# Batch 1's a*b as Strassen's block products in a fused attention and expert kernel

## The chip, the cores and the metric
The kernel runs on one core of one Trainium2 chip. The metric is the device time of one execution in microseconds. PE is TensorE, ACT ScalarE, DVE VectorE, POOL GpSimd; SP issues the DMAs.

## What is computed
The reference in short (B, H, S, D = 2, 8, 576, 64; all float32):

```
attention: local = softmax(causal(q k^T / 8)) v
           mem = (phi(q) M_prev) / (phi(q) z_prev + 1e-6),  phi(x) = max(x, 0) + min(exp(x), 1)
           x = sigmoid(beta) mem + (1 - sigmoid(beta)) local      -> 1152 x 512
first part: a = x w1;  b = x w2;  h = (a * b) w3;  x' = h w_out    (weights arrive as float64)
experts:    out = sum over e of p[:, e] * (relu(x' w1[e]) w2[e]),  4 experts, F = 1024
```

## The kernel before
Products of float32 precision are made from two fp32r numbers, a high and a low half, in three passes (PASSES: high by low, low by high, high by high). "Splitting" a tile is a cast on ACT (or POOL) and a subtraction on DVE (`lo_dve`) or POOL (`lo_pool`).

Attention runs over 8 pairs of heads, p = 0 to 7; pairs 0 to 3 are batch 0. Its steps have short names: e, f (phi), s (scores), m (row peak on DVE), x (exp on ACT), t, c (transposes on PE, copies on ACT), v (product with v), j (scaling), n, g (the memory product and its scaling), ja (the sum of both, on POOL), z, zh, zl (the transposed x, high and low half). Pairs 0 to PLAIN - 1 have their scores from plain float32 q and k; for the others q and k are split first (hq, hk on ACT, lq, lk on POOL).

Beside it the weights are converted: o units are w_out, w units the product W = w3 w_out (so h w_out is hT by W), b units the tiles of w1 and w2. Each unit has ACT operations (oa, wa, ba), joins on DVE (od, wd, bd) and splits (oh and ol; wp; bp). b<u>_<a> is batch 0's a or b for weight tile u and half a of the 576 tokens: 12 matmuls of 288 columns. bc keeps a in SBUF; rm, rh, rl multiply and split the result into hT. k and kc are batch 0's c = hT by W and its copy to x2, in two PSUM banks M0 and M1 (one for each half). As a tile of w1 or w2 is joined for batch 0 it is stored to DRAM (wf), and read again for batch 1.

The string FIRST lists these steps in an order written out by hand. Inside `tc.manual_schedule(engines=...)` the named engines execute their instructions in the program's order; what is issued outside, or on an engine not named, a planner puts between by its own costs. In FIRST, SP is not named: loads of the ring of staging buffers are issued by `ahead()` at the joins, the loads of q, k and v (loadq, loadk, head) at their steps.

Then batch 1's a*b (`BUnits`, lines 493 to 582): 16 weight tiles, each loaded from wf, split by ACT and DVE, and used in 2 x 12 matmuls of 288 columns; `times`, `h_hi`, `h_lo` make hT. In between `early` splits two of the experts' operand blocks and prepares the first expert weight set. Batch 1's c (`c1`, line 839) is issued outside the order, so the planner places it.

The expert stage (lines 919 to 962) already works by Strassen's scheme in its Winograd form: for a pair of weight tiles seven block products P1 to P7 of 6 matmuls (two k blocks, three passes), summed in the PSUM banks Z, Q and R. `prep_1` (line 744) makes the weight operands of a set from a raw tile r: hi0 to hi3 are casts on ACT, lo0 to lo3 subtractions on POOL, s31 and s24 two sums or differences each on POOL. hi0 and lo0 split A11 and A12; s31 makes S3 and S1; s24 makes S2 and S4 and overwrites the raw A11 and A12, after lo0.

Of the kernel before, what the change touches and what calls it, by code (L numbers as in the profile page):

```python
# [19 lines left out]
e0 f0 s00 s01 m00 m01 s02 x00 s03 loadq2 loadk2 m02 x01 m03 wa0 t00 t02 c00 wd0 x02 s10 wp0 c02 x03 e1 t04 m10 oa0 t01  # L20
f1 c04 s11 x10 od0 t05 s12 c01 c05 m11 t03 e2 t06 oa1 m12 v00 c03 od1 s13 loadq3 loadk3 c06 x11 v01 m13 x12 v02 head4
head5 x13 t10 oa2 j0 t11 s20 c10 od2 c11 s21 hq3 t14 m20 hk3 lq3 t12 c14 m21 c12 n0 x20 lk3 loadk5 t13 g0 v10 c13 x21
f2 v11 oh0 ja0 e3 t15 oh2 t16 s22 c15 ol0 c16 oh1 t20 m22 wa1 v12 head6 head7 t22 ol1 x22 s23 loadq4 loadk4 j1 w0_0
c20 m23 c22 t21 n1 wd1 x23 t24 c21 z0 g1 oa3 wp1 t23 w0_1 c24 c23 s30 f3 loadq5 zh0 t25 zl0 ja1 t26 e4 m30 c25 v20 c26
od3 x30 v21 ol2 wa2 s31 v22 head8 head9 m31 oh3 w0_2 j2 x31 s32 wd2 t30 z1 c30 m32 t32 wa3 ol3 zh1 n2 wd3 x32 w0_3
w1_0 c32 zl1 wp2 wa4 t34 g2 s33 c34 t33 m33 y0 ja2 n3 c33 t31 x33 w1_1 wd4 hq4 t35 c31 z2 hk4 g3 lq4 c35 t36 w1_2 zh2
w1_3 f4 loadq6 c36 wa5 v30 zl2 wp3 y1 v31 e5 wd5 v32 head10 head11 w2_0 j3 lk4 loadk6 wa6 w2_1 w2_2 f5 w2_3 w3_0 wd6
y2 w3_1 e6 w3_2 wp4 w3_3 s40 y3 ja3 oa4 w4_0 m40 w4_1 od4 x40 z3 w4_2 wp5 zh3 w4_3 oh4 zl3 s41 y4 s42 m41 wp6 wa7 w5_0
m42 x41 w5_1 w5_2 wd7 x42 w5_3 w6_0 ol4 ba0 wp7 w6_1 y5 w6_2 w6_3 bd0 w7_0 y6 w7_1 oa5 bp0 w7_2 w7_3 s43 y7 od5 b0_0
hq5 hk5 m43 lq5 loadq7 oh5 b0_1 ba1 ol5 x43 lk5 loadk7 t40 t41 bc00 n4 c40 bd1 c41 t44 bc01 t42 c44 g4 bp1 s50 oa6 t43  # L30
m50 v40 c42 c43 od6 x50 b1_0 f6 oh6 b1_1 ba2 ol6 rm00 e7 bd2 t46 t45 rh00 v41 c45 rl00 ba3 rm01 bp2 s51 rh01 m51 c46
v42 head12 head13 rl01 x51 b2_0 bd3 j4 ba4 bp3 b2_1 bc20 s52 bd4 bc21 b3_0 m52 ja4 ba5 b3_1 rm10 x52 bp4 rh10 s53 rm11
rl10 rh11 b4_0 bd5 hk6 hq6 rl11 b4_1 oa7 m53 bp5 x53 t50 bc40 t51 od7 bc41 b5_0 c50 c51 lq6 oh7 b5_1 ba6 rm20 ol7 rh20
bd6 t52 t54 c52 n5 c54 rl20 ba7 rm21 bp6 t53 g5 v50 rh21 c53 t55 rl21 bd7 b6_0 c55 f7 t56 wa8 v51 bp7 c56 bc60 b6_1
# [21 lines left out]
def kernel(  # L56
# [228 lines left out]

    def stage_b(p):
# [27 lines left out]
        def pv(x):  # L314
            def f():
                if x == 0:
                    st["a"] = slots("a")
# [8 lines left out]
            return f
# [733 lines left out]
```

## Time and profile before

| | us |
|---|---|
| median of 3 runs (696.35 to 697.58) | 697.29 |
| profiled execution | 696.56 |
| its span, first to last instruction | 694.4 |
| PE busy | 678.9 |
| DVE, ACT, POOL busy | 415.2, 371.1, 358.7 |

Attention and batch 0's a*b end near 212 us, batch 0's c is 212 to 237, batch 1's a*b 237 to 301 with most of batch 1's c between, and the experts fill the rest. PE's busy time counts matmuls that overlap in the pipeline, so a busy PE can still run at less than its rate; for a rate, starts are to be compared.

### The profile page before, as it was taken

What the parts mean: (1) busy time and instruction counts of PE and PEld (TensorE: products, weight loads), DVE (VectorE), ACT (ScalarE), POOL (GpSimd) and SP (SyncE); (2) the same over time, 40 slices, a digit from 0 to 9 for tenths busy, and PEclk for the clock granted to TensorE, in tenths of its full rate; (3) what the DMA queues carried; (4) which work ended last, traced back from release to release, by engine and by line L of the source; (5) the groups of instructions that cost most, each with busy time, mean ns of one, the idle gap of its engine ahead of it and who ended that gap; (6) DMA issues with size and microseconds to landing.
All of it is one profiled execution on the core that took longest, in us unless ns stands there. A gap on an engine that the chain in (4) does not pass through costs nothing.

```text
span 694.4 us, 12951 instructions
## 1 busy us (share of the span) xinstructions
PE 678.9 (98%) x4999; PEld 610.7 (88%) x4999; DVE 415.2 (60%) x784; ACT 371.1 (53%) x787; POOL 358.7 (52%) x352
## 2 busy tenths in 40 slices
PE   7899999999999999999999999999999999999997
PEld 4678798977999999999898999998999899999896
DVE  6689788898761044456766573455563465634563
ACT  7788686676732134445454544445544445444551
POOL 2225546565450000515767776568765768666660
PEclk9999999999999999999999999999999999999999
DMA  9743256533540013122131322131313122312501
GB/s 302 254 146 102 67 198 195 172 122 123 194 140 31 1 61 122 35 88 93 35 117 61 122 94 89 61 122 62 122 61 121 61 94 90 123 60 85 173 31 60
DMA packets 43404, 74.53 MB, mean 107 GB/s; under 512 B 14416, under 2 KB 14416, under 8 KB 43344
## 3 DMA queue, kind: packets, MB, share of 16 engines
q1 hardware_dynamic: 43344, 73.72, 32.3%
q8 instruction: 39, 0.64, 0.4%
q14 instruction: 21, 0.17, 0.1%
HBM read 67.15 MB, written 6.55 MB: 106 GB/s over the span
## 4 chain that ended last, share of the span: by engine, by line
PE 87%; DMA 4%; DVE 3%; ACT 2%; issue 1%; POOL 1%; SPq 0%; ACTq 0%; POOLq 0%; DVEq 0%
PE o L885 27%; PE Z L932 14%; PE ab L532 13%; PE c L625 7%; PE Q L932 7%; PE wacc L463 6%; PE R L932 3%; PE a L322 2%; PE pt L300 2%; DMA qd<-in_q_cols_dram 2%; PE sc L250 1%; DMA wr<-in_moe_w_tiles_dram 1%; PE b L355 1%; DVE P L266 1%; PE a L332 1%
## 5 line engine op out<-in xcount | busy, mean ns | idle before, releaser
L102 POOL TENSOR_TENSOR w<-r,w 128x512 fp32r<-128x512 f32 x96 | 131.4, 1369 | 186.6 <-ACT w L760 172.8
L885 PE MATMUL o<-w,he 128*128 128x512 f32 x864 | 223.1, 391 | 0.0
L885 PEld LDWEIGHTS o<-w,he 128*128 128x128 f32 x864 | 153.5, 188 | 23.4
L532 PE MATMUL ab<-xT,ws 128*128 128x288 f32 x768 | 107.6, 297 | 1.2 <-POOL ws L102 1.2
L870 ACT ACTIVATE he<-t 128x320 fp32r<-128x320 f32 (+1 forms) x96 | 42.7, 445 | 121.9 <-DVE t L961 74.2
L532 PEld LDWEIGHTS ab<-xT,ws 128*128 128x128 f32 x768 | 103.0, 188 | 2.9 <-POOL ws L102 1.6
L871 DVE SCALAR_TENSOR_TENSOR he<-t,he 128x320 fp32r<-128x320 f32 (+1 forms) x96 | 58.7, 611 | 49.1 <-ACT he L870 49.1
L105 DVE TENSOR_TENSOR w<-r,w 128x512 fp32r<-128x512 f32 x64 | 66.0, 1032 | 0.0
L954 DVE TENSOR_TENSOR t<-u,Q 128x320 f32<-128x320 f32 (+1 forms) x32 | 14.5, 454 | 81.4 <-ACT u L952 81.2
L760 ACT CAST w<-r 128x512 fp32r<-128x512 f32 x96 | 58.9, 614 | 0.0
L625 PE MATMUL c<-hT,W 128*128 128x288 f32 (+2 forms) x384 | 52.9, 295 | 0.0
L625 PEld LDWEIGHTS c<-hT,W 128*128 128x128 f32 x384 | 51.6, 189 | 0.0
L932 PE MATMUL Z<-X0T,w 128*128 128x320 f32 x288 | 50.3, 310 | 0.3 <-ACT s L942 0.3
L932 PEld LDWEIGHTS Z<-X0T,w 128*128 128x128 f32 x288 | 46.0, 188 | 4.2 <-ACT s L942 0.7
L463 PE MATMUL wacc<-wo,w3s 128*128 128x512 f32 x192 | 49.0, 402 | 0.0
L932 PEld LDWEIGHTS Z<-X1T,w 128*128 128x128 f32 x288 | 40.8, 188 | 3.9
L463 PEld LDWEIGHTS wacc<-wo,w3s 128*128 128x128 f32 x192 | 34.7, 188 | 8.2 <-issue 0.6
L932 PE MATMUL Z<-X1T,w 128*128 128x256 f32 x288 | 41.9, 281 | 0.0
L266 DVE CUSTOM_DVE_ANT_0 P<-sc,mask 128x128 f32<-128x128 f32 (+4 forms) x72 | 33.7, 515 | 10.2 <-PE sc L250 9.6
L790 ACT CAST w<-r 128x512 fp32r<-128x512 f32 x64 | 39.5, 618 | 0.0
L271 ACT ACTIVATE P<-P,mn 128x128 f32<-128x128 f32 (+4 forms) x72 | 37.3, 580 | 2.1 <-DVE mn L266 2.0
L99 POOL TENSOR_SCALAR w3s<-tf_l 128x512 fp32r<-128x512 f32 x16 | 11.8, 741 | 51.3 <-DVE tf_l L135 32.4
(136 smaller groups left out, 1157.8 us busy)
## 6 DMA issues: line engine op xcount, KB each, us to landing
r<-in_moe_w_tiles_dram SPq DMA_DIRECT2D x64, 256.0 KB, 3.7
r<-in_moe_w_dram SPq DMA_DIRECT2D x64, 256.0 KB, 2.9
w3r<-in_moe_w_tiles_dram SPq DMA_DIRECT2D x16, 512.0 KB, 3.7
wr<-in_moe_w_tiles_dram SPq DMA_DIRECT2D x16, 512.0 KB, 3.6
wor<-in_moe_w_out_dram SPq DMA_DIRECT2D x8, 512.0 KB, 5.0
wf<-tf SPq DMA_DIRECT2D x16, 256.0 KB, 2.2
wr<-wf SPq DMA_DIRECT2D x16, 256.0 KB, 2.8
qd<-in_q_cols_dram SPq DMA_DIRECT2D x8, 352.0 KB, 3.7
```

The costliest lines, as they stand in the source:

```text
L102: nc.gpsimd.tensor_sub(dst, src, r32(hi))
L105: nc.vector.tensor_sub(dst, src, r32(hi))
L266: nc.vector.tensor_tensor_reduce(out=Pt[i, x], in0=src, in1=mask[:, 0:S] if i == NB else mask[:, S + P - w : S + P], scale=ISCALE, scalar= ...
L463: nc.tensor.matmul(wacc[u], lhsT=w3s[u][:, a, c, :], rhs=wo[4 * g + c][:, bb, :], start=(c == 0 and x == 0), stop=(c == 3 and x == 2),)
L532: nc.tensor.matmul(ps[:, 0:HS], lhsT=self.ws[u][:, wi, kk, :], rhs=xT[b, kk][:, xi, a * HS : (a + 1) * HS], start=(n == 0), stop=(n == 3 * ...
L625: nc.tensor.matmul(st["ps"], lhsT=Wt[kk][:, wi, d * P : (d + 1) * P], rhs=hT[kk][:, xi, t0 : t0 + tw], start=(kk == 0 and x == 0), stop=(k ...
L760: return lambda: nc.scalar.copy(st["w"][i][:, 0], src(i))
L790: return lambda: nc.scalar.copy(w2s[s][x][:, 0], st["r"][:, x])
L870: nc.scalar.activation(h[:, 0], src, AF.Relu)
L871: nc.vector.scalar_tensor_tensor(out=h[:, 1], in0=src, scalar=0.0, in1=r32(h[:, 0]), op0=ALU.max, op1=ALU.subtract)
L885: nc.tensor.matmul(o_ps[i], lhsT=h_of[s][x][:, a, i * P : (i + 1) * P], rhs=w2s[s][x][:, b, :], start=first, stop=last,)
L932: nc.tensor.matmul(ps, lhsT=w1s[s][a][:, wi, kk, :], rhs=X[c, b][:, xi, kk, :], start=first and kk == 0 and x == 0, stop=(kk == 1 and x == ...
```

## The change
- FIRST is written anew, with SP's instructions in it: tokens with @ are loads (@q, @k, @V for two heads, @o, @w, @b, @mz, @bt), bs the stores to wf. SP is now one of the named engines. `gates` is a step of its own, after @bt.
- PLAIN is 4.
- The slots of a pair's nine output blocks are reordered, so that `mem` makes four products of 130 columns over 128 rows and two of 65, and the gates' tiles are smaller.
- For batch 1 `fin_hi` writes x in float32 (two tiles xf), and there is no low half.
- What stands behind the last step of FIRST that is not k (`cut_at`) is issued in a second block together with `work`: `x_b1` makes the seven token operands (B11, B21, B22, T1 to T4) of batch 1's x, and `prep_b1(0..2)` three weight sets. Two entries of `work` follow each k step.
- In that block follow, for m = 0 to 7, the seven products of pair m of weight tiles (w1's tile m is the upper block row, w2's the lower one, the two halves of 576 tokens are the block columns, so the four sums are a and b of either half), with prep_b1(m + 2) for m = 1 to 5 between them. Z and Q of even m are in M0 and M1 with R in o0; those of odd m are in o1, o2, o3.
- The raw tiles of wf have two buffers (the tags of the later blocks X0B22 and X1B22); the sets have three (the experts' v tags, and the tags of T1 to T4 of either part), so these blocks of the experts are allocated after a*b.

```diff
+@q0 @k0 @k1 @q1 e0 @V0 f0 s00 s01 @w0 m00 e1 m01 s02 x00 @o0 f1 s03 @V1 x01 m02 wa0 t00 @k2 t02 m03 @q2 s10 x02 wd0
+@w1 s11 c00 wp0 c02 t01 m10 @o1 x03 t04 c01 s12 @o2 c04 m11 x10 t03 m12 v00 @mz c03 x11 t05 @bt v01 c05 x12 t06 t10
+s13 c06 c10 e2 v02 m13 @q3 oa0 t14 gates j0 @k3 t13 c14 n0 @V2 x13 od0 t11 s20 g0 c11 @o3 wa1 t12 m20 v10 ja0 c12 c13
+x20 t16 v11 f2 oh0 wd1 t15 e3 s21 c15 ol0 @w2 c16 oa1 v12 m21 wp1 w0_0 j1 @V3 x21 s22 od1 s23 m22 t20 oa2 @w3 t22 m23
...
-PLAIN = 3
+PLAIN = 4
...
+    def slot(i, x):
+
+        return i // 2, (i % 2) * 2 + x
...
-                    nc.tensor.matmul(
-                        m[x][:, i], lhsT=phi_t[p][o, i * P : (i + 1) * P], rhs=mz[o, p, x], start=True, stop=True
-                    )
-            for x, o in enumerate(halves):
+                g, s = slot(i, 0)
                 nc.tensor.matmul(
-                    m[0][o, NB], lhsT=phi_t[p][o, NB * P : S], rhs=mz[o, p, x], start=True, stop=True
+                    m[g][:, s : s + 2], lhsT=phi_t[p][:, i * P : (i + 1) * P], rhs=mz[:, p], start=True, stop=True
+                )
+            for x in range(2):
+                nc.tensor.matmul(
+                    m[0][x * SB : (x + 1) * SB, NB], lhsT=phi_t[p][:, NB * P : S], rhs=mz[:, p, x], start=True, stop=True
                 )
 
         def mem_out():
@@ -372,23 +381,26 @@
             nc.gpsimd.tensor_add(st["q"], st["q"], st["m"])
 
...
-            nc.scalar.copy(xT[b, h // 2][:, 0, :], st["x"])
+            nc.scalar.copy(xf[h // 4][:, h // 2 % 2, :] if b else xT[b, h // 2][:, 0, :], st["x"])
 
         def fin_lo():
-            lo_dve(xT[b, h // 2][:, 1, :], st["x"], xT[b, h // 2][:, 0, :])
+            if b == 0:
+                lo_dve(xT[b, h // 2][:, 1, :], st["x"], xT[b, h // 2][:, 0, :])
 
...
+            self.raw[u] = self.flt[u] = from64_join(*self.raw[u])
+
+        def store(self, u):
             wf[u] = wd.tile([P, KD, P], F32, tag=f"f{u}", name=f"wf{u}")
-            nc.sync.dma_start(out=wf[u], in_=f)
-            ahead()
+            nc.sync.dma_start(out=wf[u], in_=self.flt.pop(u))
...
+    for c, n in (("o", KF), ("w", NU), ("b", NU)):
+        parts.update({f"@{c}{u}": lambda c=c, u=u: loads[c](u) for u in range(n)})
+    parts["@bt"] = lambda: nc.sync.dma_start(out=bt, in_=beta)
+    parts["@mz"] = lambda: nc.sync.dma_start(out=mz, in_=m_z)
...
+    cut_at = max(i for i, f in enumerate(FIRST) if f[0] != "k") + 1
+    with tc.manual_schedule(engines=ENGINES | {ET.SP}):
+        for f in FIRST[:cut_at]:
             parts[f]()
...
+    BX = {}
+    b1_raw, b1_set = {}, {}
+
+    def load_b1(m):
+        if m < KF:
+            b1_raw[m] = r = px.tile([P, 2, KD, P], F32, tag=f"X{m % 2}B22", name=f"wr1_{m}")
+            for x in range(2):
+                nc.sync.dma_start(out=r[:, x], in_=wf[2 * m + x])
+
+    def b1_tiles(m):
+        if m % 3 == 0:
+            return [px.tile([P, 2, n, P], F32R, tag=f"v{i}", name=f"b1w{i}_{m}") for i, n in enumerate(SIZES)]
+        c = m % 3 - 1
+        return [px.tile([P, 2, n, P], F32R, tag=f"X{c}{BL[2 + i]}", name=f"b1w{i}_{m}") for i, n in enumerate(SIZES)]
+
+    def prep_b1(m):
+
+        p = prep_1(m, b1_raw, b1_set, b1_tiles, "tb")
+        sub, add = nc.vector.tensor_sub, nc.vector.tensor_add
+        return [
+            lambda: (p["begin"](), p["hi0"]()), p["s31"], p["lo0"], p["hi2"], p["s24"], p["lo2"], p["hi3"], p["lo3"],
+            p["hi1"], lambda: (p["lo1"](), load_b1(m + 2)),
+        ]
+
+    def x_b1():
+
+        x0, x1 = xf
+        t = pf.tile([P, 2, HS], F32, tag="asb", name="xt", bufs=1)
+        lft, rgt = slice(0, HS), slice(HS, S)
+        b11, b12, b21, b22 = x0[:, :, lft], x0[:, :, rgt], x1[:, :, lft], x1[:, :, rgt]
+        where = {
+            "B11": (main, "g6"), "T1": (main, "g7"), "B21": (main, "g2"), "B22": (main, "g3"), "T2": (px, "X0B11"),
+            "T3": (px, "X0B21"), "T4": (main, "g4"),
+        }
+
+        def hi(n, src):
+            def f():
+                pool, tag = where[n]
+                BX[n] = pool.tile([P, 2, 2, HS], F32R, tag=tag, name=f"BX{n}")
+                nc.scalar.copy(BX[n][:, 0], src)
+            return f
+
+        def lo(n, src):
+            return lambda: lo_dve(BX[n][:, 1], src, BX[n][:, 0])
+
+        sub = nc.vector.tensor_sub
+        return [
+            hi("B11", b11), lambda: sub(t, b12, b11), lo("B11", b11), hi("T1", t), lambda: sub(b12, b22, b12), lo("T1", t),
+            hi("B21", b21), hi("B22", b22), lambda: sub(t, b22, t), lo("B21", b21), hi("T2", t), lo("B22", b22),
+            hi("T3", b12), lo("T2", t), lambda: sub(b21, b21, t), lo("T3", b12), hi("T4", b21), lo("T4", b21),
+        ]
+
+    st_m = {}
+
+    def b1_prods(m):
+
+        st_m[m] = st = {}
+        banks = ((psM, "M0"), (psM, "M1"), (ps3, "o0")) if m % 2 == 0 else ((ps3, "o1"), (ps3, "o2"), (ps3, "o3"))
+
+        def new(i):
+            pool, tag = banks[i]
+            return pool.tile([P, 512], F32, tag=tag, name=f"{'ZQR'[i]}b{m}", bufs=1)[:, 0:HS]
+
+        def prod(d, a, b, first):
+            def f():
+                if first:
+                    st[d] = new("ZQR".index(d))
+                for kk in range(2):
+                    for x, (wi, xi) in enumerate(PASSES):
+                        nc.tensor.matmul(
+                            st[d], lhsT=b1_set[m][a][:, wi, kk, :], rhs=BX[b][:, xi, kk, :],
+                            start=first and kk == 0 and x == 0, stop=(kk == 1 and x == 2), skip_group_check=True,
+                        )
+            return f
+
+        def keep(i):
+            def f():
+                if i == 0:
+                    st["u"] = pf.tile([P, 3, HS], F32, tag="ws", name=f"u{m}")
+                nc.scalar.copy(st["u"][:, i], st["Z"])
+            return f
+
+        def add(i, k, d):
+            def f():
+                if i == 0:
+                    st["t"] = pf.tile([P, 3, HS], F32, tag="raw", name=f"t{m}")
+                nc.vector.tensor_add(st["t"][:, i], st["u"][:, k], st[d])
+            return f
+
+        def fin_h(a):
+            def f():
+                t = st["t"]
+                nc.vector.tensor_mul(t[:, a], t[:, a], st["Z"] if a == 0 else t[:, 2])
+                if a:
+                    hT[m] = po.tile([P, 2, S], F32R, tag=f"o{m}", name=f"hT1_{m}")
+                    both = t[:, 0:2].rearrange("p a s -> p (a s)")
+                    nc.scalar.copy(hT[m][:, 0, :], both)
+                    lo_dve(hT[m][:, 1, :], both, hT[m][:, 0, :])
+            return f
+
+        return {
+            "P1": [prod("Z", "A11", "B11", True), keep(0)], "P2": [prod("R", "A12", "B21", True), add(0, 0, "R")],
+            "P6": [prod("Z", "S2", "T2", False), keep(1)], "P5": [prod("Q", "S1", "T1", True)],
+            "P7": [prod("Z", "S3", "T3", False), keep(2), add(2, 2, "Q")], "P4": [prod("Z", "A22", "T4", False), fin_h(0)],
+            "P3": [prod("Q", "S4", "B22", False), add(1, 1, "Q"), fin_h(1)],
+        }
+
+    tail = FIRST[cut_at:]
+    work = x_b1()
+    for m in range(3):
+        work += prep_b1(m)
     with tc.manual_schedule(engines=ENGINES | {ET.SP}):
-        for u in range(NU):
-            pre, m0, m1, post = b1.unit(u)
-            pre()
-            if u == 6:
+        load_b1(0), load_b1(1)
+        per = -(-len(work) // max(1, sum(f[1] != "c" for f in tail)))
+        for f in tail:
+            parts[f]()
+            if f[1] != "c":
+                for g in work[:per]:
+                    g()
+                work = work[per:]
+        for g in work:
+            g()
+        hT.clear()
+        early = [f for k, n in enumerate(("B11", "B21")) for f in split_x(n, 1, block(0, k, 1))]
+        p0 = prep_1(0)
+        early += [
+            lambda: (p0["begin"](), p0["hi0"]()), *(p0[n] for n in ("lo0", "s31", "hi2", "hi3", "s24", "lo2", "hi1", "lo3", "lo1")),
+        ]
+        order = [b1_prods(m) for m in range(KF)]
+        for n in ("P1", "P5", "P2"):
+            for f in order[0][n]:
+                f()
+        for m in range(KF):
+            todo = prep_b1(m + 2) if m and m + 2 < KF else []
+            if m == 4:
                 load_1(0), load_1(1)
-            m0()
-            if u >= 3 and early:
-                early.pop(0)()
-            m1()
-            post()
-            if u >= 8 and early:
-                early.pop(0)()
+            nxt = order[m + 1] if m + 1 < KF else {}
+            seq = [order[m].get("P6"), *([order[m]["P5"]] if m else []), order[m]["P7"], nxt.get("P1"), order[m]["P4"], nxt.get("P2"), order[m]["P3"]]
+            for fs in seq:
+                for f in fs or []:
+                    f()
+                for f in todo[:2]:
+                    f()
+                todo = todo[2:]
+                if early and (m == KF - 1 or m == KF - 2 and len(early) > 10):
+                    early.pop(0)()
+        x_tiles(0, BL[:2])
+        for k, n in enumerate(("B11", "B21")):
+            early += split_x(n, 0, block(0, k, 0))
...
```

## Rows read from the trace of the kernel before
**Rows 1.** Busy time by stage: stretch, length, busy of each engine (instructions), clock, DMA.
```profile
0.00:60.00 60.00, 50.09 (x589) 37.78 (x589) 45.69 (x133) 47.97 (x95) 14.43 (x25) 1.00 0.69 226
60.00:150.00 90.00, 88.85 (x848) 76.65 (x847) 75.29 (x160) 66.43 (x129) 52.81 (x45) 1.00 0.44 142
150.00:211.90 61.90, 61.62 (x594) 54.35 (x593) 46.71 (x94) 36.09 (x71) 29.77 (x28) 1.00 0.41 139
211.90:237.33 25.43, 25.43 (x194) 25.43 (x194) 1.52 (x3) 3.75 (x9) 0.00 (x0) 1.00 0.06 21
...
340.00:694.00 354.00, 350.56 (x2057) 316.13 (x2055) 192.21 (x309) 169.72 (x382) 232.70 (x229) 1.00 0.27 89
```

**Rows 2.** PE in order of time around batch 1's a*b: start, duration (us).
```profile
246.71 1.92 PE L625 MATMUL c<-hT,W 128*128 128x320 f32 x12
248.46 6.53 PE L532 MATMUL ab<-xT,ws 128*128 128x288 f32 x48
254.83 1.92 PE L625 MATMUL c<-hT,W 128*128 128x320 f32 x12
```

**Rows 3.** Waits of PE in the first 60 us: total, times, longest.
```profile
PE a L322 <- ACT pT L304: 2.0, 1, 2.0
...
PE b L355 <- DVE mn L266: 1.3, 2, 1.0
...
PE sc L250 <- DMA kd<-in_k_cols_dram: 1.0, 1, 1.0
...
PE sc L250 <- DVE mn L266: 0.8, 1, 0.8
```

**Rows 4.** ACT in order of time, 20 to 23 us.
```profile
20.84 0.68 ACT L213 ACTIVATE ex<-qd 128x576 f32<-128x576 f32 x1 [3.16 <-DMA qd<-in_q_cols_dram]
...
22.52 0.72 ACT L304 COPY pT<-pt 128x512 f32<-128x512 f32 x2
```

**Rows 5.** Groups of PE: scores with three passes (ks), plain (kd), memory product (mz).
```profile
L250 PE MATMUL sc<-ks,qs 64*128 64x128 f32 (+3 forms) x120 | 13.1, 342 | 0.0
L355 PE MATMUL b<-mz,phi 64*128 64x65 f32 x128 | 8.9, 278 | 1.3 <-DVE mn L266 1.3
L250 PE MATMUL sc<-kd,qd 64*128 64x128 f32 (+3 forms) x48 | 8.5, 465 | 1.8 <-DMA kd<-in_k_cols_dram 1.0 <-DVE mn L266 0.8
```

**Rows 6.** POOL in order of time, one set of the experts' weights.
```profile
279.83 1.89 POOL L767 TENSOR_TENSOR t<-r 128x256 f32<-128x256 f32 x2
281.68 1.43 POOL L768 TENSOR_TENSOR r<-r 128x256 f32<-128x256 f32 x2
283.07 0.73 POOL L772 TENSOR_TENSOR r<-r 128x256 f32<-128x256 f32 x1
283.88 0.86 POOL L773 TENSOR_TENSOR r<-r 128x256 f32<-128x256 f32 x1
284.70 1.29 POOL L102 TENSOR_TENSOR w<-r,w 128x512 fp32r<-128x512 f32 x1
286.15 0.75 POOL L102 TENSOR_TENSOR w<-t,w 128x256 fp32r<-128x256 f32 x1 [0.16 <-ACT w L760]
```

**Rows 7.** ACT in order of time in batch 1's a*b.
```profile
242.62 0.43 ACT L551 CAST hT<-asb 128x288 fp32r<-128x288 f32 x1 [1.15 <-DVE asb L546]
...
246.90 0.40 ACT L542 COPY asb<-ab 128x288 f32<-128x288 f32 x1 [1.20 <-PE ab L532]
247.20 0.62 ACT L523 CAST ws<-wr 128x512 fp32r<-128x512 f32 x1
```

**Rows 8.** DVE in order of time, 206 to 286 us.
```profile
206.07 0.76 DVE L105 TENSOR_TENSOR xT<-x,xT 128x576 fp32r<-128x576 f32 x1 [1.04 <-ACT xT L388]
...
242.12 0.46 DVE L546 TENSOR_TENSOR asb<-ab,asb 128x288 f32<-128x288 f32 x1
...
283.68 0.46 DVE L105 TENSOR_TENSOR hT<-asb,hT 128x288 fp32r<-128x288 f32 x1 [0.50 <-ACT hT L551]
...
285.28 1.03 DVE L105 TENSOR_TENSOR hT<-asb,hT 128x288 fp32r<-128x288 f32 x1 [0.50 <-ACT hT L551]
```

More of the change, by code (lines that the diff above doesn't have):

```diff
@@ L19 @@
 FIRST = """
[L20 to L34, printed above, removed]
@@ L646 @@
         define(p)
-        parts.update({f"load{nm}{p}": lambda nm=nm, p=p: load(nm, p) for nm in "qk"})
-        parts.update({f"head{n}": lambda n=n: load_head(n) for n in (2 * p, 2 * p + 1)})
+        parts.update({f"@{nm}{p}": lambda nm=nm, p=p: load(nm, p) for nm in "qk"})
+        parts[f"@V{p}"] = lambda p=p: (load_head(2 * p), load_head(2 * p + 1))
     for c in range(KF):
@@ L668 @@
             parts[f"kc{d}{a}"] = fs[4]
-    with tc.manual_schedule(engines=ENGINES):
-        for f in FIRST:
+    cut_at = max(i for i, f in enumerate(FIRST) if f[0] != "k") + 1
+    with tc.manual_schedule(engines=ENGINES | {ET.SP}):
+        for f in FIRST[:cut_at]:
             parts[f]()
-    b1 = BUnits(1, nc.scalar.copy, lo_dve)
-    b1.start()
     attn.close()
@@ L815, in norm_p @@
         nc.vector.tensor_mul(pr, pr, prs.unsqueeze(2).to_broadcast([P, NTT, E]))
-    hT.clear()
-    early = [f for k, n in enumerate(("B11", "B21")) for c in range(2) for f in split_x(n, c, block(0, k, c))]
-    p0 = prep_1(0)
-    early += [
-        lambda: (p0["begin"](), p0["hi0"]()), *(p0[n] for n in ("lo0", "s31", "hi2", "hi3", "s24", "lo2", "hi1", "lo3", "lo1")),
-    ]
-    with tc.manual_schedule(engines=ENGINES | {ET.SP}):
-        for u in range(NU):
-            pre, m0, m1, post = b1.unit(u)
-            pre()
-            if u == 6:
-                load_1(0), load_1(1)
-            m0()
-            if u >= 3 and early:
-                early.pop(0)()
-            m1()
-            post()
-            if u >= 8 and early:
-                early.pop(0)()
+    BX = {}
@@ L846 @@
     px.tile([P, SHIFT], F32, name="gapy")
+    for c in range(2):
+        x_tiles(c, (*BL[2:], "B22"))
     c1_rest = [f for d in range(KD) for f in c1(d, 1, (KD + d) % 5)]
@@ L1035 @@
     last = _np.repeat(beta.T[:, None], 64, 1).reshape(128, 4, 1)
-    both = [_np.broadcast_to(beta[:, x : x + 1], (128, 4, 4)) for x in range(2)]
-    inputs["beta_slots"] = _np.concatenate([both[0], last, both[1]], -1)
+    inputs["beta_slots"] = _np.concatenate([_np.broadcast_to(_np.tile(beta, 2), (128, 4, 4)), last], -1)
     inputs["moe_w3_tiles"] = inputs["moe_w3"].T.reshape(2, 4, 128, 8, 128).transpose(0, 3, 2, 1, 4).reshape(16, 128, 512)
```

141 lines of the change are left out of this document (58 added, 83 removed).

## The prediction
> **What bounds the kernel now.** I read the busy time by stage first [rows 1]. TensorE (PE) is busy 50.1 of the first 60 us, 88.9 of the next 90, 61.6 of the next 61.9, and all of the 25.4 us of batch 0's c. So it waits mostly in the first minute of the trace, while the pipeline of scores, softmax and transposes fills; from there on it is the bound. The granted clock is 1.00 in all stages, so nothing is to be had there. PE's instructions in order of time [rows 2], read from start to start (the durations overlap in the pipeline), give the rate: 48 matmuls of batch 1's a*b, one pair of weight tiles, take 254.83 - 248.46 = 6.37 us, 0.1327 each, with 12 matmuls of the later c (1.75) between. Eight pairs make 51.0 us, without a gap. ACT, DVE and POOL have much room there; POOL is idle in batch 0's c [rows 1].
>
> **The first 212 us: reordered loads and attention.** The waits of PE up to 60 us [rows 3] are 2.0 us of L322 for ACT's pT, 1.0 for kd's DMA, 0.8 of scores for DVE's mn, and 1.3 (two waits, longest 1.0) of L355 for mn. The ACT queue tells where the 2.0 comes from [rows 4]: exp of pair 2's q stood 3.16 us for its DMA, and the copies of pT at 22.52 stood behind it. The DVE work behind that is late too, which I take for the 1.0 of L355. In the new order q and k of pairs 0 and 1 go first, the gates (which need the beta load) leave the head of ACT's and DVE's queues, and e2 moves behind s13, c06 and c10, with q2 loaded earlier. I take away 2.0 + 1.0 + 0.8 + 1.0 = 4.8 us. Nothing else here is late enough to price: bounds are below.
>
> Pair 3 plain: L250 costs 13.1/5 = 2.62 us a pair with the three passes and 8.5/3 = 2.83 plain [rows 5], +0.2; for the last block (L239) I add the same again, an estimate: +0.4 in all. It frees POOL of two subtractions and ACT of two casts, which wait for nothing on PE's path now. The memory product: now 16 + 4 instructions a pair, of 65 columns on 64 rows; then 8 + 4, the 8 with 130 columns on 128 rows. Rows show L355 at 8.9/128 us busy, but no instruction of that new shape. Lower bound: half of L355's 1.1 us a pair is saved, 4 us over 8 pairs; upper bound: twice the columns cost twice, nothing is saved and nothing lost. I take 0, since the columns sum to the same. Slots reordered, the store taken out of `join`: no instruction more or fewer on PE. Dropping the low half of batch 1's four xT frees DVE, off the path.
> So this stage: -4.8 + 0.4 = **-4.4 us**. Bounds: PE's idle here is 60 - 50.1 = 9.9 in the first 60 and 1.4 in the rest [rows 1], of which the 2 us before the first matmul stay: -9.3, and -13 with the memory product's 4. On the other side SP now executes loads strictly as written; one load put behind a wait too many costs about what a landing costs (3.2 us of exposed DMA in [rows 4]): +4.
>
> **Batch 0's c and batch 1's a*b.** Removed from PE: 7 block products of 6 matmuls are 42 a pair for 48, so 8 x 6 x 0.1327 = 6.4 us. One product is 6 x 0.1327 = 0.80 us. What it adds is POOL work and order. `prep_b1` puts on POOL per pair three subtractions of 128x512 (1.29), one of 128x256 (0.75), and four 128x256 sums and differences (0.95, 0.72, 0.73, 0.86) [rows 6]: 7.9 busy; each start follows the last about 0.04 before its end, so **7.6 us a pair** (8.1 in the experts' stage: 232.7 us for 229 instructions, eight to a set [rows 1]; 7.3 if all four sums take 0.73). PE's share of a pair is 42 x 0.1327 = 5.6. So POOL is slower than PE, 61 us against 45.
>
> Whether that shows depends on how they are tied. ACT's queue is in order [rows 4], and in the new block it holds, in m's turn: keep1(m), hi0, hi2 of set m+2, keep2(m), hi3, hi1 of m+2, then the cast of hT(m), keep1(m+1). hi2 waits for POOL's s31 of the set, hi1 for s24. So P4(m), which accumulates in the bank that keep2(m) reads, cannot start before POOL has begun set m+2: the lead of three prepared sets is of no use.
> From c's start, in us: x_b1 is 12 DVE operations of 576 columns (0.76 [rows 8]); nine of them stand before ACT's hi0(0), which comes at about 9, so POOL's first lo0 starts at 9.7. Then set 0 ends at 15.7, s31(1) 17.25, s24(1) 20.05, s31(2) 24.8. ACT's output copy kc20 stands behind hi1(1): 20.05 + 0.62 + 0.40 [rows 7] = 21.05, and k30, which wants that bank at 6 x 3.18 = 19.1, is 1.95 late. kc21 stands behind hi3(2): 24.8 + 0.62 + 0.3 + 0.4 = 26.1, where k31 wants to start at 24.2: 1.85 late. c ends at 29.25 for 25.44: **+3.8**.
> Then a*b. P1, P5, P2 (2.4), P6(0) and a wait for keep1 (PE's end to copy 246.90 - 246.71 = 0.19, copy 0.40 [rows 2, 7]), then five products: P3(0) ends at 37.0. From P3's end to the next P7 the chain is 0.19 + add 0.46 + product and hand-over 0.50 + cast 0.62 + keep1 0.40 = 2.2 [rows 7, 8], covered by P6 and P5 for 1.6: 0.6 lost for each m. keep1(1) ends at 39.2, hi0(3) at 39.8, and POOL, idle since 32.4, starts lo0(3). A cycle later, 47.4, it has done s31(4); hi2 0.62 and keep2 0.40 let P4(2) start at 48.4, where PE alone would be at 47.0. From there POOL sets the pace: P4(5) at 48.4 + 3 x 7.6 = 71.2. No set is prepared after that: the rest is 15 products, 11.9, two hT waits of 0.6 and one of 0.6 for the last keep2, 13.7: end at 84.9. The planner may fill these 1.8 with d = 0 of the later c, whose bank is free by then; I take half: 84.0. Before: 25.4 + 51.0 = 76.4. So **+7.6 us** in place of -6.4. Bounds: POOL at 7.3 and all filled, +5.5; POOL at 8.1 and nothing filled, +12.
>
> One operation of DVE bears on it: hT's subtraction of 128x288, two inputs in SBUF, took 0.46 alone and 1.03 at 285.28, while POOL's subtraction ran from 284.70 to 285.99 [rows 6, 8]. The Trainium skill (SBUF — State Buffer, Who interferes with whom) says that a VectorE instruction with two SBUF inputs and a GpSimd instruction that reads SBUF exclude each other for the whole instruction. The 1.03 agrees with it. In this change the second product of hT is such an operation, in the chain above; that is the second rival.
>
> What follows is unchanged: the later c's 96 matmuls of column part 0 now come behind a*b rather than between, 14 us either way, and cover the last hT; POOL has set 0 of the experts ready about 10 us after P3(7) began, before those 14 us are over. The experts' 350 us lose and gain nothing.
>
> **Sum.** The profiled execution took 696.56 us (span 694.4, 2.2 around it; 0.7 under the median of 697.29). 696.56 - 4.4 + 7.6 = 699.76: **699.8 us**.
>
> **Rivals.**
> *No tie (faster).* POOL and ACT run far enough ahead that neither kc nor keep waits for them: c stays 25.4, a*b is 44.6 plus the hT and keep waits, 9 x 0.6, = 50.0. Then -1.0 and -4.4: 691.2. For it: POOL has nothing else to do in c [rows 1]. Against it: 61 us of POOL from c's ninth microsecond on do not fit into 76 once it has to wait for PE's turns. It decides where kc20 ends: before c + 19.1 us, this rival; after, the forecast. 0.18.
> *Lock.* The second product waits for POOL each time. Between, where POOL sets the pace, 1.4 us of slack hide the 0.57; in the three turns where PE does, up to 0.57 each: +1.7, 701.5. For it the 1.03; against it, at 283.68 the same operation took 0.46, though POOL was subtracting then too. 0.10.
> *The fill gains more.* The new order takes all 9.3 us of idle, the tie costs as forecast: 699.8 + 4.4 - 9.3 + 0.4 = 695.3. For it: ACT and DVE are busy only 48.0 and 45.7 of the first 60. Against: the pairs' chains are as long as before. 0.16.
> *SP held up.* A load in the stated order waits for a buffer and the loads behind it with it; the 4.8 are not gained: 704.6. Against: each ring load stands behind the join that frees its buffer. 0.13.
> The forecast keeps 0.43, and its own range is 697.5 to 703.
>
> **How the numbers follow.** A measurement here can tell about 0.2% (1.4 us) from no change, that is 695.9 to 698.7. Faster: all of the first rival, 0.13 of the third, 0.01 of the forecast: 0.32. Same: 0.06 of the forecast, 0.03 each of the last two: 0.12. Slower: the rest, 0.56. The range from 690 to 706 takes in the first and the last rival; a fill and no tie together (686) or both upper bounds (712) are left out.
>
> **What would show it.** In the profile after: c of batch 0 with two gaps of about 2 us before k30 and k31, their releaser ACT's x2 copy; POOL nearly solid from c + 10 to the end of a*b with one hole of some 7 us after the third set; in a*b PE waiting for ACT's u copy, and ACT for POOL's differences; turns of 7.6 us for m = 3 to 5. In the first 60 us PE's idle at about 5 in place of 9.9. The prediction is wrong if c and a*b together take under 77 us, or if c starts before 203 or after 212.

## The result and the profile after

707.19 us median (706.78 to 707.66), against 696.82 for the kernel before on the same chip: a ratio of 1.0144, 95% interval 1.0127 to 1.0162. The direction is as forecast, the size is not: +10.4 us where +3.2 were worked out, outside the range. The profiled execution took 706.78 us (span 704.8). Cut at the same places of the trace as in the prediction:

| stage | before | after | forecast change | measured change |
|---|---|---|---|---|
| start of batch 0's c | 211.72 | 208.81 | -4.4 | -2.9 |
| c of batch 0 | 25.44 | 30.72 | +3.8 | +5.3 |
| batch 1's a*b without the later c's matmuls in it | 50.9 | 56.9 | +3.8 | +6.0 |
| first o to the last matmul's start | 368.61 | 370.68 | 0 | +2.1 |

The third row is the a*b's length less 84 matmuls of the later c at 0.146 us before (63.20 - 12.26), and 42 after (63.04 - 6.13). An a*b ends 0.8 us behind the start of its last product; a wait of PE behind that is not in it.

Busy time of each engine by stage, after (the answer to [rows 1]; columns: window, its length, then busy us of PE, weight load, DVE, ACT, POOL, with the granted clock, DMA share and GB/s):

```profile
0.00:60.00 60.00, 54.20 (x576) 39.58 (x577) 46.68 (x138) 48.49 (x95) 16.01 (x25) 1.00 0.65 206
208.81:239.52 30.71, 25.96 (x194) 25.49 (x193) 9.64 (x13) 12.45 (x26) 21.04 (x23) 1.00 0.24 85
239.52:302.56 63.04, 53.47 (x380) 51.12 (x379) 27.54 (x47) 25.84 (x57) 45.89 (x48) 1.00 0.16 51
```

PE idles 5.8 of the first 60 us for 9.9, but 4.8 in c and 9.6 in a*b, where it idled none. PE in order of time (start, length, then in brackets the idle time ahead and who ended it; to be held against [rows 2]):

```profile
208.81 19.24 PE L587 MATMUL c<-hT,W 128*128 128x288 f32 x144
231.26 3.42 PE L587 MATMUL c<-hT,W 128*128 128x288 f32 x24 [3.21 <-ACT x L596]
236.22 3.46 PE L587 MATMUL c<-hT,W 128*128 128x288 f32 x24 [1.54 <-ACT x L596]
239.52 0.97 PE L854 MATMUL Zb<-BXB,b1w 128*128 128x288 f32 x6
...
256.47 1.06 PE L854 MATMUL Zb<-BXT,b1w 128*128 128x288 f32 x6 [0.95 <-ACT u L864]
...
259.56 1.06 PE L854 MATMUL Zb<-BXT,b1w 128*128 128x288 f32 x6 [1.23 <-ACT u L864]
...
264.73 1.06 PE L854 MATMUL Zb<-BXT,b1w 128*128 128x288 f32 x6 [0.92 <-ACT u L864]
```

The two gaps of c are where they were forecast, before k30 and k31, and their releaser is the copy to x2. From 256.47 to 264.73 is one turn: 8.26 us, where POOL was to allow 7.6. ACT in c shows why the copies come late:

```profile
227.46 0.62 ACT L728 CAST b1w<-wr 128x512 fp32r<-128x512 f32 x1 [3.26 <-POOL wr L736]
...
230.29 0.62 ACT L728 CAST b1w<-wr 128x512 fp32r<-128x512 f32 x1 [1.91 <-POOL wr L741]
230.81 0.39 ACT L596 COPY x<-c 128x288 f32<-128x288 f32 x1
...
234.95 0.62 ACT L728 CAST b1w<-wr 128x512 fp32r<-128x512 f32 x1 [3.23 <-POOL wr L736]
```

kc20 (230.81) stands behind hi1(1), a cast that waits for POOL's s24 (L741). POOL over one turn of a*b (its set before stood in [rows 6]):

```profile
258.52 1.26 POOL L104 TENSOR_TENSOR b1w<-wr,b1w 128x512 fp32r<-128x512 f32 x1
...
261.37 1.29 POOL L104 TENSOR_TENSOR b1w<-wr,b1w 128x512 fp32r<-128x512 f32 x1
262.63 0.73 POOL L104 TENSOR_TENSOR b1w<-tb,b1w 128x256 fp32r<-128x256 f32 x1
263.32 1.48 POOL L104 TENSOR_TENSOR b1w<-wr,b1w 128x512 fp32r<-128x512 f32 x1
264.76 1.24 POOL L735 TENSOR_TENSOR tb<-wr 128x256 f32<-128x256 f32 x1
266.08 0.73 POOL L736 TENSOR_TENSOR wr<-wr 128x256 f32<-128x256 f32 x1
266.77 1.26 POOL L104 TENSOR_TENSOR b1w<-wr,b1w 128x512 fp32r<-128x512 f32 x1
```

POOL is solid: 8.25 us from one lo0 to the next. Two of the eight are longer than their kind, 1.48 for 1.29 and 1.24 for 0.74. Beside these two, and beside POOL's first two operations in c (s31 of set 0, 0.77 and 1.14 us from 211.04), stand these of DVE:

```profile
211.13 1.30 DVE L107 TENSOR_TENSOR BXB<-xf,BXB 128x576 fp32r<-128x576 f32 x1
212.36 1.29 DVE L832 TENSOR_TENSOR xf<-xf,xf 128x576 f32<-128x576 f32 x1
...
262.75 0.93 DVE L877 TENSOR_TENSOR t<-t 128x288 f32<-128x288 f32 x1
264.41 1.00 DVE L107 TENSOR_TENSOR hT<-t,hT 128x576 fp32r<-128x576 f32 x1 [0.74 <-ACT hT L881]
```

### The profile page after: what moved, and what is told of

Same layout as the page of the kernel before. It is cut to its first block, busy times and chain, and to the rows that moved or that the text cites. A ratio compares the mean times of both kernels' runs of the same rounds, so it can differ in the third digit from the quotient of the medians.

```text
span 704.8 us, 12797 instructions
## 1 busy us (share of the span) xinstructions
PE 679.2 (96%) x4877; PEld 605.2 (86%) x4877; DVE 425.0 (60%) x791; ACT 382.7 (54%) x808; POOL 417.9 (59%) x414
## 4 chain that ended last, share of the span: by engine, by line
PE 79%; DVE 7%; POOL 5%; ACT 4%; issue 3%; DMA 1%; DVEq 0%; POOLq 0%; ACTq 0%; SPq 0%
PE o L985 27%; PE Z L1032 14%; PE Q L1032 7%; PE wacc L473 6%; PE ab L537 6%; PE c L587 4%; PE R L1032 3%; POOL b1w L104 3%; PE Zb L854 2%; PE a L330 2%; PE pt L307 2%; PE sc L253 2%; DVE P L269 1%; ACT P L274 1%; POOL tb L735 1%
## 5 line engine op out<-in xcount | busy, mean ns | idle before, releaser
L971 DVE SCALAR_TENSOR_TENSOR he<-t,he 128x320 fp32r<-128x320 f32 (+1 forms) x96 | 57.2, 596 | 49.1 <-ACT he L970 49.1
L537 PE MATMUL ab<-xT,ws 128*128 128x288 f32 x384 | 56.0, 299 | 1.4 <-POOL ws L104 1.0
L537 PEld LDWEIGHTS ab<-xT,ws 128*128 128x128 f32 x384 | 51.7, 188 | 3.4 <-POOL ws L104 2.4
L104 POOL TENSOR_TENSOR b1w<-wr,b1w 128x512 fp32r<-128x512 f32 x24 | 31.9, 1328 | 14.5 <-ACT b1w L728 14.5
```

The source lines that it names most:

```text
L104: nc.gpsimd.tensor_sub(dst, src, r32(hi))
L537: nc.tensor.matmul(ps[:, 0:HS], lhsT=self.ws[u][:, wi, kk, :], rhs=xT[b, kk][:, xi, a * HS : (a + 1) * HS], start=(n == 0), stop=(n == 3 * ...
L971: nc.vector.scalar_tensor_tensor(out=h[:, 1], in0=src, scalar=0.0, in1=r32(h[:, 0]), op0=ALU.max, op1=ALU.subtract)
```

## The experiments

Two theories stood first. One: POOL's work on the sets, tied to PE through ACT's queue, costs all of it. The other: part of it lies elsewhere (the reordered first stage, the experts). The ratios below are to the kernel before on the chip of that run; stage times are cut as above.

**e1: low halves of batch 1's sets on DVE.**

```diff
-    def prep_1(s, raw=raw1, out=w1s, tiles=None, nm="t1"):
+    def prep_1(s, raw=raw1, out=w1s, tiles=None, nm="t1", lo_on=lo_pool):
...
-        p = prep_1(m, b1_raw, b1_set, b1_tiles, "tb")
+        p = prep_1(m, b1_raw, b1_set, b1_tiles, "tb", lo_dve)
```

> The changed kernel, but the four subtractions (lo0 to lo3) of batch 1's eight weight sets go to DVE; POOL keeps s31 and s24, some 3 us a set. Theory A (POOL's work per set, handed on to PE by ACT's ordered queue, costs the time): c is back near 25.5 us, a*b near 51 to 53 with the hT waits left, time 707.2 - 10 = 697 (695 to 700). Rival B (the waits of a turn for hT and keep are the cost, POOL only happens to be busy): 705 to 707. Rival C (DVE takes POOL's place, its subtractions stand before the sums that free Q and make hT): 701 to 704.

697.19 us (696.58 to 697.49), ratio 1.0001 [0.9992, 1.0011]: 10.0 us back, by theory A. c takes 26.16 us with one gap, a*b 51.5. PE, c and two of the turns:

```profile
228.14 6.62 PE L587 MATMUL c<-hT,W 128*128 128x288 f32 x48 [0.46 <-ACT x L596]
...
258.60 1.05 PE L854 MATMUL Zb<-BXT,b1w 128*128 128x288 f32 x6 [1.09 <-ACT u L864]
...
265.53 1.05 PE L854 MATMUL Zb<-BXT,b1w 128*128 128x288 f32 x6 [1.09 <-ACT u L864]
```

A turn is 6.93 us, not PE's 5.6: the wait is still for ACT's u copy, in a queue that waits for DVE now.

**e3: each output copy of c right behind its own matmuls.** From k20 on, a kc stands ahead of the casts of the sets in ACT's queue.

```diff
-        for f in tail:
+        i20 = tail.index("k20_0")
+        for f in tail[:i20]:
...
+        ks = lambda d, a: [f"k{d}{a}_{q}" for q in range(4)] + [f"kc{d}{a}"]
+        for unit, n in (([ "kc11"] + ks(2, 0), 8), (ks(2, 1) + ks(3, 0), 8), (ks(3, 1), 99)):
+            for f in unit:
+                parts[f]()
+            for g in work[:n]:
+                g()
+            work = work[n:]
```

> The changed kernel, but from k20 on ACT's output copies kc stand right behind their own four k steps, and the casts and POOL work of prep_b1 behind them; nothing else moves. Theory A (kc waits behind casts that wait for POOL, and POOL then stands idle 7.8 us behind the third set, so it has room): the two gaps in c, 3.2 and 1.5 us, go, all behind moves up, time 702.5 (701.5 to 704). Rival (POOL's sum of work alone sets the end of a*b): a*b takes longer by what c gains, 706.5 to 707.5.

704.5 us (703.48 to 705.67), ratio 1.0113 [1.0098, 1.0128], between the two. c is whole:

```profile
209.30 25.60 PE L587 MATMUL c<-hT,W 128*128 128x288 f32 x192
234.73 0.96 PE L854 MATMUL Zb<-BXB,b1w 128*128 128x288 f32 x6
236.52 1.06 PE L854 MATMUL Qb<-BXT,b1w 128*128 128x288 f32 x6 [0.83 <-ACT x L596]
...
239.38 1.06 PE L854 MATMUL Zb<-BXT,b1w 128*128 128x288 f32 x6 [1.00 <-ACT u L864]
```

The 5.3 us that c had lost are gone, but 2.4 of them come back as waits at the head of a*b (59.3 for 56.9): keep0 and the last kc now stand behind the casts. So both theories hold a part. The three turns at POOL's pace stay at 8.27 us.

**e4: the old a*b, all else of the change** (the reordered first stage, PLAIN 4, the stores; batch 1's x keeps its low half).

```diff
+    b1 = BUnits(1, nc.scalar.copy, lo_dve)
+    b1.start()
...
-        order = [b1_prods(m) for m in range(KF)]
...
+        for u in range(NU):
+            pre, m0, m1, post = b1.unit(u)
```

> The changed kernel with the old a*b of batch 1 (16 weight tiles, 2 x 12 matmuls, splits on ACT and DVE, the low halves of xT made in attention as before) and the experts' operand blocks at their old addresses; FIRST, SP's order, pair 3 plain, slots and the smaller gate tiles stay. If the new a*b with its preparation costs the time: 696.8 - 2.9 = 694 where the 2.1 us that the experts' stage lost come from the operand blocks' addresses, 696 where they come from the 128 bytes by which the smaller gate tiles move all else. Rival (the new order of loads and attention costs it): 703 to 707.

696.52 us (696.01 to 697.27), ratio 0.9996 [0.9987, 1.0005]: the new a*b with its preparation costs all of the loss. c starts at 210.10, 1.6 earlier than before, and the experts' stage takes 370.35, 1.7 longer, so that the first stage's gain is lost again there. The next two runs are about that stage, which the prediction had at 0.

**e5: a 128-byte filler.** The smaller gates' tiles move what lies behind them by 128 bytes.

```diff
+    main.tile([P, 32], F32, name="gapg")
     pr = main.tile([P, NTT, E], F32, name="pr")
```

> The changed kernel with a filler of 128 bytes a partition behind the smaller gate tiles, so that the weights, the accumulators and hidden tiles of the experts' stage lie at their old addresses again; the operand blocks stay at their new ones. If the filler restores it, the experts' stage takes 372.8 us for 374.9 and the time is 705.1; if the operand blocks' addresses are the cause, 707.2.

707.17 us (706.41 to 707.79), ratio 1.015 [1.0135, 1.0165]; the experts take 370.12. The filler alone isn't it. By the addresses in the built programs it puts back the weight sets that had moved, the hidden tiles and the sums (192 modulo 512 bytes, for 64 after the change), but 12 of the 14 operand blocks X still lie at 448 modulo 512 where they lay at 416.

**e6: e4 and the filler together**, so that all of the experts' buffers lie as before. The edit is e5's, on e4.

> The old a*b with the rest of the change (as in e4) and a 128-byte filler, so that every buffer of the experts' stage lies where it lay before the change. Theory A (the experts' stage is slower because its buffers moved): from first o to the last matmul 368.6 us as before, in place of 370.35 in e4; 694.8 us in all (694.2 to 695.5). Rival (something else of the change slows the experts' matmuls): 370.3 again, 696.5 us.

695.05 us (694.68 to 695.3) on a chip where the kernel before took 698.14: ratio 0.9958 [0.9944, 0.9973], theory A. First o of the stage and last group of eight matmuls, before, after, and in e6:

```profile
321.56 0.63 PE L885 MATMUL o<-w,he 128*128 128x512 f32 x2
...
688.58 1.98 PE L885 MATMUL o<-w,he 128*128 128x512 f32 x8
```

```profile
329.88 0.61 PE L985 MATMUL o<-w,he 128*128 128x512 f32 x2
...
698.97 1.98 PE L985 MATMUL o<-w,he 128*128 128x512 f32 x8
```

```profile
319.76 0.63 PE L881 MATMUL o<-w,he 128*128 128x512 f32 x2
...
686.78 1.98 PE L881 MATMUL o<-w,he 128*128 128x512 f32 x8
```

367.02, 369.09 and 367.02 us, with the same matmuls in them. So where the operands lie costs 2.07 us; moving what the gates' tiles shift (e4) costs 1.74 alone, moving X (e5) 1.51 alone. Why the rate depends on the addresses is not shown.

**e10: no second input from SBUF in hT's last steps.**

```diff
-                nc.vector.tensor_mul(t[:, a], t[:, a], st["Z"] if a == 0 else t[:, 2])
+                nc.vector.tensor_mul(t[:, a], t[:, a], st["Z"])
...
-                    lo_dve(hT[m][:, 1, :], both, hT[m][:, 0, :])
+                    nc.vector.tensor_sub(hT[m][:, 1, :].rearrange("p (a s) -> p a s", a=2), t[:, 0:2], st["Z"].unsqueeze(1).to_broadcast([P, 2, HS]))
```

> The changed kernel, but hT's second product and its subtraction take the bank of P4's sum as second input in place of a buffer in SBUF (leaves out the right gate and the low half of batch 1's hT; same number of instructions of the same sizes). Theory A (VectorE instructions with two SBUF inputs and GpSimd's exclude each other, and this makes POOL's set 8.25 us in place of the 7.6 of the prediction): POOL's set 7.6 us, a*b shorter by about 3 us, 704 us in all (703 to 705). Rival (POOL's instructions are as long without that): set 8.2 us, 706.5 to 707.5.

706.51 us (706.13 to 706.91), ratio 1.0124 [1.0106, 1.0143]. POOL's set falls to what the sum of its parts said:

```profile
258.27 1.26 POOL L104 TENSOR_TENSOR b1w<-wr,b1w 128x512 fp32r<-128x512 f32 x1
...
263.07 1.29 POOL L104 TENSOR_TENSOR b1w<-wr,b1w 128x512 fp32r<-128x512 f32 x1
264.32 0.74 POOL L735 TENSOR_TENSOR tb<-wr 128x256 f32<-128x256 f32 x1
265.14 0.74 POOL L736 TENSOR_TENSOR wr<-wr 128x256 f32<-128x256 f32 x1
265.83 1.26 POOL L104 TENSOR_TENSOR b1w<-wr,b1w 128x512 fp32r<-128x512 f32 x1
```

7.56 us a set, and a*b 54.8 for 56.9. The mechanism is theory A's: beside POOL's operations hT's product and subtraction now take 0.45 and 0.75, and neither engine's are longer than alone. (The subtraction also no longer waits for ACT's cast, but POOL's set does not hang on that.) Of its 3 us 2.1 came in a*b; 0.8 of them are lost right behind it, where PE waits for DVE. In the ratio the gain is 0.2%, and the two intervals overlap, so the exclusion is shown by the trace and not by the time.

**e9: pair 3 in three passes again.** The casts and subtractions of pair 4 had to move behind pair 3's scores, since they share their tiles.

```diff
-PLAIN = 4
+PLAIN = 3
...
-x20 t16 v11 f2 oh0 wd1 t15 e3 s21 c15 ol0 @w2 c16 oa1 v12 m21 wp1 w0_0 j1 @V3 x21 s22 od1 s23 m22 t20 oa2 @w3 t22 m23
+x20 t16 v11 f2 oh0 wd1 t15 e3 s21 hq3 c15 hk3 lq3 ol0 @w2 c16 oa1 v12 m21 wp1 w0_0 j1 @V3 x21 lk3 s22 od1 s23 m22 t20 oa2 @w3 t22 m23
```

> The changed kernel with pair 3's scores in three passes again (its four casts and subtractions put back; pair 4's moved behind pair 3's scores). Theory A (plain scores cost the 0.4 us that the prediction priced): batch 0's c starts 0.4 us earlier than the 208.8 of the changed kernel, 706.8 us in all. Rival 1 (plain pair 3 is the whole 1.2 us of busy time that TensorE gained ahead of c): 207.6 and 706.0. Rival 2 (plain bought cover in the fill, the casts come late without it): later than 208.8, 707.5 to 709.

710.02 us (709.29 to 711.24), ratio 1.018 [1.0155, 1.0205]; c starts at 211.35, 2.5 later. Rival 2. The longest wait of PE ahead of c that is new (columns: us in total, times, longest):

```profile
PE b L364 <- DVE mn L269: 2.0, 1, 2.0
```

The scores' groups are busy 30.7 us for 31.6, so plain scores cost PE 0.9 us; but they spare the fill two casts and two subtractions, and PE idles 10.4 us ahead of c in this run for 7.2. The run moved pair 4's as well, so that the 2.5 us are not pair 3's alone.

**e7: e1, and hT's last steps behind keep1 of the next turn.**

```diff
-            "P3": [prod("Q", "S4", "B22", False), add(1, 1, "Q"), fin_h(1)],
+            "P3": [prod("Q", "S4", "B22", False), add(1, 1, "Q")], "F": [fin_h(1)],
...
-            seq = [order[m].get("P6"), *([order[m]["P5"]] if m else []), order[m]["P7"], nxt.get("P1"), order[m]["P4"], nxt.get("P2"), order[m]["P3"]]
+            seq = [order[m]["P6"] + (order[m - 1]["F"] if m else []), *([order[m]["P5"]] if m else []), order[m]["P7"], nxt.get("P1"), order[m]["P4"], nxt.get("P2"), order[m]["P3"]]
```

> On top of e1 (low halves of batch 1's sets on DVE), the second product and the cast and subtraction of hT(m) are written behind P6 and keep1 of turn m+1. Theory A (once POOL no longer sets the pace, the turn is P3, add, product, cast, keep1, P7 in ACT's order, 1.3 us over PE's 5.6): turns of 6.9 fall to about 6.1 us, a*b falls by 4 to 5 us, 693 us in all (692 to 694.5). Rival (DVE, busy 5.9 of a 6.9 us turn, is the next bound): turns stay at 6.6 to 6.9 and the time at 695.5 to 697.5.

695.88 us (695.59 to 696.9), ratio 0.9975 [0.9965, 0.9985]. The rival, by the turns: 6.79 us, and the wait is as long as it was, now for keep2. (The time lies in the rival's range too, but on a chip where the kernel before takes 698.14.)

```profile
259.90 1.06 PE L854 MATMUL Zb<-BXT,b1w 128*128 128x288 f32 x6 [0.93 <-ACT u L864]
...
266.69 1.08 PE L854 MATMUL Zb<-BXT,b1w 128*128 128x288 f32 x6 [0.96 <-ACT u L864]
```

**e8 and e8b: e1, e3, hT's last steps behind keep2, and fillers for the old addresses modulo 512; in e8b one subtraction of four (lo1) back on POOL.**

```diff
+    main.tile([P, 32], F32, name="gapg")
...
-    px.tile([P, SHIFT], F32, name="gapx")
...
+            if m == 0:
+                px.tile([P, SHIFT], F32, name="gapx")
...
+                px.tile([P, 128 - SHIFT], F32, name="gapz")
```

> What the runs so far point to, together: low halves of batch 1's sets on DVE (e1), each output copy of c right behind its own matmuls (e3), hT's last steps written behind keep2 of the next turn, and fillers that put the experts' operands back on the addresses (modulo 512 bytes) that they had before the change. Theory A: c 25.4; turns of a*b 6.0 to 6.3 us, set by DVE's 6 us of work a turn; c and a*b together 72 to 74 us in place of 77.7 in e1; experts' stage 368.6 as before; 690 us in all on a chip where the kernel before takes 696.8 (688.5 to 692). Rival (the remaining tie through ACT's queue keeps turns at 6.8): 693 to 694.

> As e8, but one of the four subtractions of a set (lo1, 128x512) back on POOL, which is idle for most of a turn then. Theory A (DVE's work sets the turn): 0.2 to 0.6 us a turn shorter than e8, 1 to 3 us in all. Rival (DVE and POOL exclude each other, so that moving it gains nothing): within 0.7 us of e8.

e8: 694.99 us (694.28 to 695.88), ratio 0.9971 [0.9961, 0.9982], above both ranges. c is 25.44 and the experts' stage 368.72, as expected; a*b is 50.6, and its turns are 7.01 us, nearer to the rival's 6.8. One turn's busy time (columns as above), then DVE at its end:

```profile
260.85:267.86 7.01, 6.11 (x43) 5.64 (x43) 6.27 (x11) 3.64 (x9) 3.83 (x5) 1.00 0.31 110
```

```profile
265.89 0.91 DVE L882 TENSOR_TENSOR t<-t 128x288 f32<-128x288 f32 x1
267.54 0.76 DVE L107 TENSOR_TENSOR hT<-t,hT 128x576 fp32r<-128x576 f32 x1 [0.74 <-ACT hT L886]
268.21 1.23 DVE L107 TENSOR_TENSOR b1w<-wr,b1w 128x512 fp32r<-128x512 f32 x1
```

DVE is busy for 6.27 of the 7.01 us, as theory A had it, and for the other 0.74 it waits for ACT's cast of hT, which is the rival's tie: together they are the turn. DVE's work is itself longer beside POOL's: 0.91 here for 0.46, 1.23 for the 0.69 of the same subtraction with POOL idle in e1 (266.03).

e8b: 696.12 (695.57 to 697.13), ratio 0.9989 [0.998, 0.9999]; a*b 52.1, 1.5 more.

```profile
237.59 1.07 PE L859 MATMUL Qb<-BXT,b1w 128*128 128x288 f32 x6 [1.29 <-ACT x L597]
...
261.75 1.06 PE L859 MATMUL Zb<-BXT,b1w 128*128 128x288 f32 x6 [0.89 <-ACT u L869]
...
268.51 1.07 PE L859 MATMUL Zb<-BXT,b1w 128*128 128x288 f32 x6 [0.91 <-ACT u L869]
```

Its turns are shorter, 6.76 us, by the 0.25 that its theory A allowed. What it loses stands at the head of a*b: the last copy of c is behind a cast that waits for POOL again, and the first three products take 1.8 us longer than in e8.

e6, e7 and e8 beat both kernels, the one before by 0.25 to 0.42%. The fastest by the ratio, e6, does without the block products, but its interval overlaps that of e8.

## Why the prediction was too low

*Mechanism.* The first rival, no tie, is refuted by the gaps of c and by e1; the forecast's chain (output copies and u copies behind casts that wait for POOL) is what the trace shows, with POOL's hole ahead of the fourth set at 7.77 us where some 7 were named. What failed are four terms of the sum, 7.2 us together (10.2 measured between the profiled executions for 3.2, and 0.2 less time around the span, 2.0 us for 2.2).

1. *POOL's set of 7.6 us in batch 1's products: mis-sized, +2.2.* With DVE's two-input operations beside it, a set takes 8.25: the three turns at POOL's pace are 2.0 longer than forecast, P4(2) starts 0.9 later into a*b, and the rest is 0.7 shorter. For POOL alone the price was right (7.56 in e10, 7.62 and 7.49 between the lo0 of the first three sets in c), but in part by luck: it took sums of 0.95 and 0.86 that were themselves long, and took off an overlap. In e10 the four sums take 0.74 each and the set is 7.56 all the same, where the prediction's bound for that case was 7.3. The prediction had seen the lengthening on DVE's side (1.03 for 0.46, [rows 8]) and priced it there, as slack that hides it. But POOL's operations lengthen too, and POOL is the engine that sets the turn. [rows 6] held that side as well: the first two differences there took 1.89 us together where the next two took 1.43, and beside the first two stood this DVE operation with two inputs in SBUF:

```profile
280.33 0.78 DVE L105 TENSOR_TENSOR ws<-wr,ws 128x512 fp32r<-128x512 f32 x1 [1.64 <-ACT ws L523]
```

   With the exclusion gone (e10) a*b measured 54.8 us where the prediction's chain gives 84.0 - 29.25 = 54.75, and P4(2) starts 19.3 us into it, for 48.4 - 29.25 = 19.15. The Trainium skill (SBUF — State Buffer, Who interferes with whom) says that a VectorE instruction with two SBUF inputs contends with a GpSimd instruction that reads SBUF, by an exclusive lock on a shared pair of ports. e10 agrees with it, by 0.69 us a set. So the rival named Lock held the cause, with 1.7 us on the wrong engine and a chance of 0.10.
2. *c of batch 0, +3.8: mis-sized, +1.5.* k30 starts 3.37 us late (3.21 of them idle) for 1.95; k31 1.78 late for 1.85. POOL's first lo0 starts at c + 10.95, not 9.7, and two of the nine operations of x_b1 ahead of it took 1.30 and 1.29 where 0.76 was counted: 1.07 of the 1.25. They stand beside the two operations of POOL's first s31; that it is the same exclusion is likely by the trace and e10, but no run took it away in c.
3. *First stage, -4.4: +1.5.* PE's idle time ahead of c fell by 4.1 us (11.3 to 7.2) where 4.8 were named, and its busy time rose by 1.2 (200.4 to 201.6) where 0.4 was priced. PE's waits of the first 60 us after (for [rows 3]; the 2.0 us ahead of the first matmul stay and are left out):

```profile
PE a L330 <- DVE mn L269: 1.4, 1, 1.4
PE a L330 <- DVE xm L356: 0.9, 1, 0.9
PE pt L307 <- ACT pT L311: 0.6, 1, 0.6
```

   The 2.0 for pT and kd's DMA are gone, and mn and xm are late next. The scores' groups are busy 31.6 us for 30.2 in all, +1.4 where 0.4 was priced for pair 3; 0.9 of it goes with three passes (e9), at the price of longer waits. The memory product was rightly 0: 8.7 + 2.7 us busy for 8.9 + 2.7. With the same first stage, c began between 208.4 and 209.9 in the eight kernels after, e1, e3, e5, e7, e8, e8b and e10 (e4, with batch 1's low halves in it: 210.1), so about 1 us of it is not settled.
4. *The experts, 0: missed, +2.1.* Not an instruction of them changed, but their buffers moved, by tiles that became smaller and blocks allocated later (e4 to e6). The prediction didn't look at addresses.

The 6 matmuls of 48 are gone from PE (its own c and a*b would be 25.4 + 44.6 = 70.0 us), but PE waits for POOL through ACT, and none of the 6.4 us is seen. With the subtractions moved (e1), 10.0 us come back and the changed kernel stands level with the one before; with c's order and the addresses mended too (e8) it is 2 us ahead.

## What to carry to other kernels

When work moves to an idle engine, price its set with what its neighbour does to it at that moment, and put every such lengthening on the engine that sets the pace, not on the one where it was seen. A queue in order ties any short copy to the slowest producer ahead of it; writing the copy first gave back about half here (5.3 us in c, 2.4 of them lost again behind it), since the producer stayed the bound. Where a change alters the size or the place of buffers, hold the addresses of the untouched stage against the old ones before trusting a 0 there.

## What the runs showed of the hardware

- The same matmuls on the same data sizes took 367.02 or 369.09 us in the experts' stage, by where weights, operand blocks and sums lie (shifts of 128 and 32 bytes modulo 512). The profiles of one placement agree within 0.11 us (before, e6, e8, e8b; after, e1, e3, e7, e9, e10). The 864 matmuls of 512 columns took 199.95 us for 198.41, start to start.
- Both sides of an exclusion pay: hT's second product took 0.93 for 0.46, POOL's subtraction beside it 1.48 for 1.29; hT's subtraction took 1.00 for 0.76, POOL's difference beside it 1.24 for 0.74. (In the first turn of a*b, with POOL idle, DVE's two took 0.46 and 0.76.) With DVE's second input from PSUM, in e10, all four took their shorter time.
- After the wait of 3.2 us in c, PE's granted clock stayed at 1.00 (2.4 GHz) in the profiles of after and e9; in that of e10, after the same wait, it was 0.54 over the next 3.75 us, nearly all of them at the lower level (1.2 GHz), and in that of e5 0.57 over the next 4:

```profile
228.00:231.75 3.75, 0.54 (x5) 0.30 (x3) 0.00 (x0) 1.84 (x5) 3.59 (x4) 1.00 0.31 118
231.75:235.50 3.75, 3.75 (x16) 3.75 (x17) 0.00 (x0) 0.54 (x2) 3.67 (x6) 0.54 0.17 38
```

  It cost nothing there, since the second half of c would have waited 1.54 us for its bank anyway: c took 30.7 us in both.
